# Attention sums on 32x32 tiles, with sequence quarter and head on the partitions and v kept on the chip

## The chip, the core and the metric

One core of a Trainium2 chip runs the kernel. Its engines work at the same time, each on its own instructions in their written order: TensorE (PE in the profile; its weight loads are shown as PEld), VectorE (DVE), ScalarE (ACT), GpSimd (POOL) and SyncE (SP), whose queue issues nearly all transfers. They meet through semaphores. The metric is the device time of one execution in microseconds; the time before is the median of three runs.

## What is computed

Two independent parts, whose outputs stand side by side in one result of 2048 x 1152, bfloat16. Part A is attention of 32 heads of 18 columns, in which each position looks at 8 earlier positions two apart (a window with dilation). Part B is a short convolution of k, a product with v, a causal convolution over the whole sequence (by a Fourier transform), and a product with q.

```python
def _A_ref(x, wqkv, wo):                   # x 1 x 2048 x 576
    H = 32; Dh = D // H; W, dil = 8, 2
    q, k, v = qkv[0], qkv[1], qkv[2]       # of x @ wqkv, by head
    idx = pos[:, None] - off[None, :]      # off = 0, 2, ..., 14
    mask = idx >= 0
    logits = jnp.einsum("bhsd,bhswd->bhsw", q, kg) * scale
    logits = jnp.where(mask[None, None, :, :], logits, -1e9)
    attn = _softmax(logits, axis=-1)
    o = jnp.einsum("bhsw,bhswd->bhsd", attn, vg)
    return o.transpose(0, 2, 1, 3).reshape(B, S, D) @ wo

def _B_ref(q, k, v, shift_k, ssm_k, ssm_D):
    # k_shift: 4 taps of shift_k over k; kv = k_shift * v
    # y: causal convolution of kv with ssm_k, by FFT of length 2 S
    y = y + kv * ssm_D[None, None, :]
    return q * y
...
return jnp.concatenate([a, b], axis=-1)
```

## The kernel before

**Order.** A string `ORDER` lists some 500 steps by short names with numbers, and a loop at the end calls the function of each; that is the order in which every engine and every queue gets its instructions. A suffix after a colon chooses the PSUM pool (`a` or `b`, two buffers of 2 x 512 fp32 each) and the engine that copies out of PSUM (`s` for ACT, `v` for DVE). So a step's place in the string decides what stands ahead of it on each engine, and an instruction that waits holds up what is behind it on its engine.

**Part A.** `load_x`, `x_tr` bring x in and transpose it on PE. `qk_step` and `qk_tail_step` project q and k, with the columns (head, element) on the partitions and all 2048 positions in the row. `v_step(c, k)` projects v for 512 positions in the same way, with 16 columns from the chunk before in front, and writes it to a DRAM buffer `Dv`; `v_load` reads it back with another layout: partition (head, j), where j = 0..3 is a window offset, and elements of v and positions in the row. Four of the eight windows lie in the partitions, the other two groups of four (`wg`) are made by an offset.

`l_mul(n, h)` multiplies q with shifted k on DVE (4096 elements in a row of each partition; the remaining 64 columns have products of 2048). `l_sum(n)` adds over the elements of a head with PE: a matrix `Eh` of zeros and ones, 32 columns wide, on one of four column tiles of the array (`tile_position=(0, 32 * j)`), so that partition (j, head) of `Lt` gets the logits of window j. `at_step` transposes these on PE so that positions lie on the partitions, `softmax(hf, k)` runs in twelve steps for each half of the sequence (maximum in three steps, difference, exponential on ACT, sum in three steps, reciprocal, conversion, product in two steps), `bt_step` transposes back. `p_mul(c, ct)` multiplies the weights with v for chunk c of 512 positions and four (for ct = 4 two) elements of each head; `p_sum(c, k)` adds over the windows with a matrix `I4` on column tiles, and `p_out(c, tt)` is the output projection with `wo`. The output of two `p_out` leaves in one transfer, from one of two staging buffers.

**Part B.** `load_k`, `load_v`, `sk_step`, `kv_conv` (on DVE, products and sums of 2304 elements), `x_part` and `k_part` (first stage of the transform on PE, results to DRAM buffers `Dx`, `Dk`), `w_load` (back from there), `x_spec` and `k_spec` (second stage, line 594), `g_prod` (the complex product on DVE, two products of 1152 elements for each of 16 steps, lines 615 and 616), `g_inv` (inverse, line 629, to `Dy`), `y_load`, `y_step` (last stage on PE, product with q on DVE, line 706, result out).

**Buffers.** All work areas are cut by hand from ten `Area` tiles, re-used as the kernel goes on. A `Ring` is a set of slots; a step that takes a slot waits for its last user. `evac` and `copy32` are the helpers that copy from PSUM: lines 103, 105 and 367 in the profile stand for all of them.

Of the kernel before, what the change touches and what calls it, by code (L numbers as in the profile page):

```python
# [18 lines left out]
lx.0 tj lx.1 lx.2 lwq.1 lwv wm.11 tv t0 xt.0.2:av sk:b lk.0 t2 xt.1.2:av lwq.0 xt.1.0:av xt.1.1:bv xt.0.0:s xt.0.1:bv  # L19
xt.2.1:s qk.1.1.1:bs xt.2.2:s t3 tw t1 lx.3 cv.0.0:a lv.1 lk.1 qk.1.1.0:bs cv.0.1:b cv.0.2:b cv.0.3:b qk.1.0.0:s  # L20
xt.2.0:as lv.0 v.0.1:b cv.0.4:b v.1.1:bs wt lk.3 v.0.0:a xt.3.0:s cv.0.5:b lk.2 cv.0.6:a cv.0.7:b cv.1.0 qk.0.1.0:b
xt.3.1:b t4 xt.3.2:as cv.1.1 lm.0.1 cv.1.2:b t5 cv.1.3:b qk.0.0.0:a sx.0.0:s qt.1:s cv.1.4:a lm.0.0 v.2.1:as lv.2
sx.1.0:a cv.1.5 cv.1.6 sx.0.1:b qt.0:b sx.0.2:a cv.1.7:a qk.0.1.1 sx.1.1 qk.0.1.3:b v.0.2:s v.1.2:bs lm.0.2 v.1.0:a
sx.1.2:b qk.1.0.1:bs sx.3.0:b cv.2.0:a qk.0.0.1:a v.3.1:a cv.2.1 sx.3.1 sx.2.0:s cv.2.2:a qt.3:as v.2.0:as qk.1.1.3:bs
sx.2.1:s cv.2.3:a lm.1.0 lb.0:a cv.2.4 cv.2.5:b v.2.2:bs cv.2.6 lm.1.1 v.3.2:av sx.2.2:b sx.3.2:b lv.3 cv.2.7:b
qk.0.1.2:a lb.1:b cv.3.0:b lm.2.2 cv.3.1 cv.3.2:b v.3.0:a qk.1.1.2:bs lm.2.1 qk.0.0.3:bs qk.1.0.3:bs lwo sx.4.0:a
cv.3.3:a lm.3.1 qt.2 sx.4.1:b sx.4.2 qk.0.0.2:as cv.3.4:b cv.3.5:b sx.5.0:b lm.2.0 qk.1.0.2 sx.5.1:a lb.2:bs cv.3.6
cv.3.7:a lm.6.0 at.0.0 lkn sx.5.2:av lm.4.2 ia:b lm.3.0 sx.6.0:as sx.6.1:as sx.6.2:s kt.3:b sx.7.0 sx.7.1:a sx.7.2:av
kt.1:bv lb.3:bs kp.1.0:bs kp.1.1:as lm.4.1 lm.4.0 kp.1.2:bs kp.3.0:s kt.0:as kp.3.1:b kp.3.2:s lm.6.2 kt.2:av lb.4:a
kp.0.0 kp.0.1:s lm.6.1 at.0.1 sm.0.0 xl.0 kp.0.2 kp.2.0:av lm.5.1 kp.2.1:s kp.2.2:bs kt.5:as kt.4:s sm.0.1 lb.6:a  # L30
kp.5.0:av kp.5.1:bs lm.5.0 sm.0.2 xl.1 kp.5.2:as kp.4.0:bs kt.6 kp.4.1:a kp.4.2:as sm.0.3 kt.7:s lb.5:s kp.6.0:as
xs.0.0:bv kp.6.1:a xl.2 kp.6.2:as kp.7.0:v kp.7.1:a kp.7.2 lm.7.0 sm.0.4 lm.7.1 xs.1.0:as sm.0.5 xs.0.1 xs.1.1:a
sm.0.6 lb.7:bs sm.0.7 kl.1 sm.0.8 kl.0 kl.3 ks.1.0:s sm.0.9 sm.0.11 sm.0.10 ks.1.1:as ks.0.0 gp.1.0 at.1.0:av vl.0.0
gp.1.1 bt.0.1:v ks.0.1:bs gp.0.0 ks.3.0:bs gi.1.0:as vl.0.1 xs.2.0:b xl.4 xs.2.1:as gp.0.1 xl.3 bt.0.0:bv at.1.1:b
vl.1.2 sm.1.0 ks.3.1:as kl.2 gi.1.1 pm.0.0 gi.0.0:s xs.3.0:a sm.1.1 vl.0.2 ks.2.0:b pm.0.1 xs.3.1:as sm.1.2 gp.3.0
vl.1.0 kl.4 sm.1.3 gi.0.1:bs gp.3.1 pm.0.2 xs.4.0:as gp.2.0 ks.2.1:b ps.0.0:a pm.0.3 sm.1.4 ks.4.0:b xl.7 gp.2.1 kl.7
gi.3.0:a ks.4.1:b gp.4.0 xs.4.1:as vl.1.1 gi.2.0:s pm.1.4 ks.7.0:a xl.5 pm.1.0 ps.0.1:bs ks.7.1:s vl.2.0 gp.4.1 pm.1.1
xs.5.0:as sm.1.5 sm.1.6 xs.7.0:b kl.6 kl.5 gi.2.1:a xs.7.1:bs ps.1.0:v xs.5.1:b ks.5.0:a vl.3.0 xl.6 gi.4.0 ps.1.2:a
gi.3.1:s vl.3.2 pm.1.2 gi.4.1:as ks.5.1:s pm.0.4 sm.1.7 gp.5.0 pm.1.3 sm.1.8 ps.0.2:bs gp.5.1 xs.6.0 yl.3 sm.1.9 yl.2
ps.1.1:a ks.6.0:s po.0.0:s xs.6.1:bs sm.1.10 gi.5.0:a gp.7.0 yl.0 vl.2.1 gi.5.1:bs gp.6.0 po.0.2:a sm.1.11 vl.2.2  # L40
gp.7.1 po.0.1 ys.3.0:v ys.3.1:v yl.1 bt.1.1:as bt.1.0 po.0.3:bs ks.6.1:bs pm.2.0 gi.7.0:as gi.7.1 gp.6.1 pm.2.1
gi.6.0:a po.1.0:bs pm.2.2 ps.2.0:a vl.3.1 gi.6.1:bs pm.2.4 ys.2.0:av ps.2.2:bs pm.2.3 ys.0.0:v ys.2.1:bs ys.0.1:as
po.1.2 ps.2.1:a po.1.1:b po.1.3:bs pm.3.4 pm.3.0 po.2.0 yl.6 yl.4 pm.3.1 po.2.1:s ps.3.0:b pm.3.2 ps.3.2:a po.2.2:b
pm.3.3 ys.6.0:as yl.5 ys.1.0:v ys.1.1:v ps.3.1:as ys.6.1:v po.2.3:v yl.7 po.3.0:a ys.5.0:bv ys.5.1:a po.3.1:b po.3.2:s
ys.4.0:v po.3.3:b ys.4.1:v ys.7.0:a ys.7.1:bs
# [4 lines left out]
def kernel(  # L50
# [62 lines left out]
    Dv = dram.tile([4 * D, VT], BF16, name="Dv")  # L113
# [40 lines left out]
    class Ring:  # L154
# [27 lines left out]
    wv = const.tile([128, 6, D], BF16, name="wv")  # L182

    r1, r2, r3, r4, r5, r6, r7, r8, r9, r10 = (
        Area(f"area{i}", n) for i, n in enumerate((18528, 16384, 5 * S, 2560, 5 * 2 * D, 19 * D, 28 * D, 2 * S, 3168, 4 * D)))
# [11 lines left out]
    Lt = r8.take(2, S)  # L197
    vTs = [[r9.take(2, VT) for _ in range(2)], [r9.take(2, VT), r10.take(2, VT)]]
    wqt = r10.take(5, 2, 64)
    vtl = [r10.take(272) for _ in range(2)]  # L200
    for r in (r1, r3, r4, r5, r6, r7, r9, r10):
        r.reset()
# [6 lines left out]
    ath = [r5.take(8, W, H) for _ in range(2)]  # L209
    smt = r5.take(1536)  # L210
    Pr = Ring(*[r1.take(2, 4, 512) for _ in range(3)])
    Ptr = Ring(r1.take(2, 2, 512))
    oTr = Ring(r9.take(2304), r1.take(2304))
    sAr = Ring(r1.take(2, D))
# [4 lines left out]
    Yr = Ring(r7.take(8, HD), r7.take(8, HD))  # L219
    qtr = Ring(*[r7.take(4, HD) for _ in range(4)])  # L220
    Pp = Ring(r4.take(4, 2, HD), *[r7.take(4, 2, HD) for _ in range(3)])
    r7.reset(20 * D)
    shr = r7.take(4 * D)[0:1]
# [3 lines left out]
    prr = Ring(*[mk.take(4, 2, 512) for _ in range(3)])  # L227
    phr = Ring(mk.take(4, 512), mk.take(4, 512))
    mk.reset()
    vSr = Ring(*[mk.take(8, VT) for _ in range(3)])  # L230
    vStr = Ring(mk.take(2, VT), mk.take(2, VT))
    mk.reset()
# [21 lines left out]
    def load_wv():  # L254
        nc.sync.dma_start(wv[:, 0:4, :], A_wqkv[0:512, 2 * D:3 * D].rearrange("(kb p) a -> p kb a", p=128))
        nc.gpsimd.memset(wv[0:64, 4:6, :], 0.0)
        nc.sync.dma_start(wv[64:128, 4, :], A_wqkv[512:576, 2 * D:3 * D])
# [9 lines left out]
    wot = wv  # L267
    wor = A_wo.rearrange("(h d) n -> h d n", d=DH)

    def load_wo():  # L270
        for r in range(4):
            nq = 5 if r < 2 else 4
            nc.sync.dma_start(wot[32 * r:32 * r + 32, 0:nq, :], wor[:, r:r + 4 * nq - 3:4, :])
        nc.gpsimd.memset(wot[64:128, 4, :], 0.0)
        for r in range(2):
            nc.sync.dma_start(wot[32 * r + 64:32 * r + 96, 5, :], wor[:, 16 + r, :])

    ones_f, ident_f, i4_f = mk.f32(128), mk.f32(128), mk.f32(32)
# [19 lines left out]
    def t_ident():  # L298
        nc.gpsimd.memset(ones_f, 1.0)
        affine_pair(ident_f, ones_f, pattern=[[1, 128]], cm=-1, base_lo=0, base_hi_minus=0)  # L300
        nc.vector.tensor_copy(ident[:], ident_f)
        affine_pair(i4_f, ones_f[:, 0:32], pattern=[[-4, 32]], cm=1, base_lo=0, base_hi_minus=3)
        nc.vector.tensor_copy(I4[:], i4_f)
# [79 lines left out]
    def v_step(c, k):  # L383
        ps = psa()
        r0 = D * c + 256 * k
        if k < 2:
            vT, nxt = vTs[k][c % 2], vTs[k][1 - c % 2]
            if c == 0:
                nc.gpsimd.memset(vT[:, :, 0:16], 0.0)
            project(ps, wv, (256 * k, 256 * k + 128), slice(512 * c, 512 * c + 512))  # L390
            evac(vT[:, :, 16:VT], ps[:])
            nc.sync.dma_start(Dv[r0:r0 + 256, :].rearrange("(u p) t -> p u t", p=128), vT)
            if c < 3:
                nc.gpsimd.tensor_copy(nxt[:, :, 0:16], vT[:, :, 512:VT])
            return
        vt, nxt = vtl[c % 2], vtl[1 - c % 2]
        if c == 0:
            nc.gpsimd.memset(vt[0:64, 0:16], 0.0)
        for kb in range(5):
            for hh in range(2):  # L400
                t0 = 512 * c + 256 * hh
                nc.tensor.matmul(ps[64 * hh:64 * hh + 64, 0, 0:256], wv[:, kb, 512:D], xT[:, kb, t0:t0 + 256],
                                 start=(kb == 0), stop=(kb == 4), tile_position=(0, 64 * hh))
        evac(vt[:, 16:272], ps[:, 0, 0:256])
        nc.sync.dma_start(Dv[r0:r0 + 64, 0:272], vt[0:64, :])
        nc.sync.dma_start(Dv[r0:r0 + 64, 272:VT], vt[64:128, 16:272])
        if c < 3:
            nc.gpsimd.tensor_copy(nxt[0:64, 0:16], vt[64:128, 256:272])

    def v_load(c, k):  # L410
        nd = 8 if k < 2 else 2
        dst = (vSr if k < 2 else vStr).get((c, k))
        sl = Dv[D * c + 8 * k:D * c + 8 * k + 1, 2:3]
        nc.sync.dma_start(dst.rearrange("p d t -> p (d t)")[:, 0:nd * VT - 8],
                          bass.AP(tensor=sl.tensor, offset=sl.offset, ap=[[DH * VT, 32], [DIL, 4], [1, nd * VT - 8]]))
# [93 lines left out]

    def block(n):  # L510
        return n // 2 % 2, n // 4, 2 * (n // 4) + n % 2

    def l_mul(n, h):
        wg, m, aq = block(n)
        o0 = PADL - DIL * (W - 1 - 4 * wg)
# [121 lines left out]
    def p_mul(c, ct):  # L637
# [5 lines left out]
        if ct % 2:  # L643
            vSr.drop((c, ct // 2))
# [110 lines left out]
```

## Time and profile before

| what | value |
| --- | --- |
| time, median of 3 runs | 233.52 us (232.54 to 233.6) |
| profiled execution, span | 233.3 us |
| instructions | 4423 |
| PE busy, matmuls | 196.2 us (84%), 1727 |
| PEld busy, weight loads | 112.5 us (48%), 1736 |
| DVE busy | 200.7 us (86%), 199 |
| ACT busy | 164.7 us (71%), 241 |
| POOL busy | 22.2 us (10%), 53 |
| DMA, all queues | 60.57 MB, mean 260 GB/s |
| mean granted TensorE clock | 0.954 |

The span runs from the first to the last instruction of the profiled execution. Busy time of an engine is the time in which at least one of its instructions ran; matmuls are pipelined, so many lie in the same microsecond, and the mean duration of one says little of what the next has to wait. In a row of a group the number behind x counts the instructions, then come the busy time in us and the mean of one in ns, and after the second bar the time that the engine stood idle just before them. In the 40 slices a digit is the busy share in tenths, 9 for 90% or more. In the rows of stretches each engine has its busy us and in brackets its instructions; the last three numbers are the granted clock, the share of DMA engine time and GB/s. In a timeline row the first number is the start in us from the span's start, the second the us to the end of the last of the merged instructions. In the rows of the chain the numbers are start and length in us.

### The profile page before, as it was taken

What the parts mean: (1) busy time and instruction counts of PE and PEld (TensorE: products, weight loads), DVE (VectorE), ACT (ScalarE), POOL (GpSimd) and SP (SyncE); (2) the same over time, 40 slices, a digit from 0 to 9 for tenths busy, and PEclk for the clock granted to TensorE, in tenths of its full rate; (3) what the DMA queues carried; (4) which work ended last, traced back from release to release, by engine and by line L of the source; (5) the groups of instructions that cost most, each with busy time, mean ns of one, the idle gap of its engine ahead of it and who ended that gap; (6) DMA issues with size and microseconds to landing.
All of it is one profiled execution on the core that took longest, in us unless ns stands there. A gap on an engine that the chain in (4) does not pass through costs nothing. (4 is left out here: it accounts for less than half of the span.)

```text
span 233.3 us, 4423 instructions
## 1 busy us (share of the span) xinstructions
PE 196.2 (84%) x1727; PEld 112.5 (48%) x1736; DVE 200.7 (86%) x199; ACT 164.7 (71%) x241; POOL 22.2 (10%) x53
## 2 busy tenths in 40 slices
PE   7899969999999977959873979668898979896981
PEld 2644524544544444545532456434564656564661
DVE  2679999989596999778969999999999999996533
ACT  2675739677754969487989789899999758535321
POOL 8001540110210110200000000000000010010100
PEclk9999999999999996779998599999999999997999
DMA  6999823451169589977996998999798999799586
GB/s 221 348 276 393 248 85 106 155 162 48 55 198 268 134 273 327 218 221 211 307 290 207 330 353 326 374 355 400 306 360 299 327 332 379 274 275 339 121 272 214
DMA packets 46965, 60.57 MB, mean 260 GB/s; under 512 B 2368, under 2 KB 40064, under 8 KB 45920
## 3 DMA queue, kind: packets, MB, share of 16 engines
q1 hardware_dynamic: 46254, 57.78, 75.5%
q0 software_dynamic: 688, 2.51, 4.6%
q8 instruction: 13, 0.21, 0.4%
q14 instruction: 8, 0.07, 0.1%
q10 hardware_dynamic: 2, 0.00, 0.0%
HBM read 38.98 MB, written 21.31 MB: 258 GB/s over the span
## 5 line engine op out<-in xcount | busy, mean ns | idle before, releaser
L103 ACT ACTIVATE area<-psB 128x576 bf16<-128x576 f32 (+7 forms) x122 | 85.2, 745 | 32.2 <-PE psB L381 7.6
L103 ACT ACTIVATE area<-psA 128x576 bf16<-128x576 f32 (+7 forms) x105 | 75.6, 760 | 30.7 <-PE psA L381 12.0
L519 DVE TENSOR_TENSOR area<-area 128x4096 bf16<-128x4096 bf16 x16 | 36.4, 2285 | 5.7 <-PE psA L540 3.3
L642 DVE TENSOR_TENSOR area<-area,area 128x4096 bf16<-128x4096 bf16 (+1 forms) x20 | 40.7, 2069 | 0.1
L381 PEld LDWEIGHTS <-area 128*128 128x128 bf16 x160 | 15.5, 98 | 20.0 <-issue 3.0
L594 PEld LDWEIGHTS <-W 128*64 128x64 bf16 x256 | 14.1, 113 | 22.0 <-issue 15.0
L484 DVE TENSOR_TENSOR area<-area,area 128x2304 bf16<-128x2304 bf16 x16 | 21.6, 1362 | 0.8 <-PE psB L456 0.6
L594 PE MATMUL psB<-area,W 128*64 128x288 bf16 x160 | 16.2, 299 | 6.9 <-DMA area<-Dk 3.9
L381 PE MATMUL psB<-area,area 128*128 128x512 bf16 x85 | 20.1, 379 | 0.3
L693 POOL DMA_DIRECT2D area<-in_B_q_dram x8 | 6.0, 747 | 142.8 <-DVE area L706 119.2
L381 PE MATMUL psA<-area,area 128*128 128x512 bf16 x67 | 16.1, 379 | 2.7 <-DVE area L367 2.5
L456 PE MATMUL psB<-area,T 128*128 128x384 bf16 x58 | 14.8, 346 | 2.9 <-ACT area L103 2.7
L456 PEld LDWEIGHTS <-T 128*128 128x128 bf16 x96 | 9.3, 104 | 15.1 <-issue 9.2
L486 DVE TENSOR_TENSOR area<-area,area 128x2304 bf16<-128x2304 bf16 x12 | 16.3, 1356 | 0.3
L629 PEld LDWEIGHTS <-IAt 64*128 64x128 bf16 x256 | 12.4, 94 | 6.9 <-issue 4.0
L680 PEld LDWEIGHTS <-area 128*128 128x128 bf16 x128 | 12.4, 100 | 5.8 <-issue 2.6
L381 PE MATMUL psA<-area,wv 128*128 128x512 bf16 x60 | 13.9, 379 | 0.0
L594 PE MATMUL psA<-area,W 128*64 128x288 bf16 x96 | 10.2, 310 | 4.1 <-ACT area L103 3.6
L381 PEld LDWEIGHTS <-wv 128*128 128x128 bf16 x80 | 7.6, 98 | 9.4 <-issue 0.6
L616 DVE TENSOR_TENSOR area<-area 128x1152 bf16<-128x1152 bf16 x16 | 12.0, 749 | 0.0
L615 DVE TENSOR_TENSOR area<-area 128x1152 bf16<-128x1152 bf16 x16 | 11.9, 746 | 0.0
L456 PE MATMUL psA<-area,T 128*128 128x384 bf16 x38 | 10.0, 364 | 1.8 <-ACT area L103 1.7
(132 smaller groups left out, 270.1 us busy)
## 6 DMA issues: line engine op xcount, KB each, us to landing
area<-Dv SPq DMA_DIRECT2D x8, 1054.0 KB, 8.0
Dx<-area SPq DMA_DIRECT2D x16, 288.0 KB, 3.6
Dk<-area SPq DMA_DIRECT2D x16, 288.0 KB, 3.5
area<-Dx SPq DMA_DIRECT2D x8, 576.0 KB, 5.7
area<-Dk SPq DMA_DIRECT2D x8, 576.0 KB, 5.3
Dy<-area SPq DMA_DIRECT2D x8, 576.0 KB, 4.6
area<-Dy SPq DMA_DIRECT2D x8, 576.0 KB, 7.0
out_dram<-area SPq DMA_DIRECT2D x16, 288.0 KB, 3.7
```

The costliest lines, as they stand in the source:

```text
L103: nc.scalar.activation(dst, src, ACT.Copy, **({} if scale is None else {"scale": scale}))
L381: nc.tensor.matmul(ps[:, u, :], w[:, kb, cols[u]:cols[u] + 128], xT[:, kb, t], start=(kb == 0), stop=(kb == 4))
L456: nc.tensor.matmul(ps[:, ri, 0:384], T1[:, ri, :], sf[:, 384 * ch:384 * ch + 384], start=True, stop=not extra)
L484: nc.vector.tensor_tensor(tB if k else tA, kfull[:, 4 * c + 3 - j:4 * c + 7 - j, :], skb[:, j, :].unsqueeze(1).to_broadcast([128, 4, D]), ...
L486: nc.vector.tensor_tensor(tA, tA, tB, ALU.add)
L519: nc.vector.tensor_tensor(prr.get((n, h)), q2[h][:, :, 512 * aq:512 * aq + 512].unsqueeze(1).to_broadcast([128, 4, 2, 512]), kv, ALU.mult)
L594: nc.tensor.matmul(ps[64 * hp:64 * hp + 64, im, 0:HD], W2[:, im, 8 * g + 2 * prl + hp].rearrange("p l f -> p (l f)"), Wt[:, 2 * prl + hp, ...
L615: nc.vector.tensor_tensor(P[:, 0:2], X, K, ALU.mult)
L616: nc.vector.tensor_tensor(P[:, 2:4], X, swap, ALU.mult)
L629: nc.tensor.matmul(ps[:, hp, 0:HD], IAt[r, tab, 4 * g + 2 * hv + u, :], Pp[(i, hv)][r, n, u, :], start=(n == 0), stop=(n == 3), tile_posit ...
L642: nc.vector.tensor_tensor(P, vv, Lt[:, :, 512 * c:512 * c + 512].unsqueeze(2).to_broadcast([128, 2, nd, 512]), ALU.mult)
L680: nc.tensor.matmul(ps[:, di, 0:288], oT[:, 512 * ct + 128 * tt:512 * ct + 128 * tt + 128], wot[:, ct, d0:d1], start=(ct == 0), stop=False)
```

## The change

The attention gets another layout. Partition (a, head), where a = 0..3 is a quarter of the sequence of 512 positions, holds logits, softmax and v; the eight windows lie in the row. `l_sum(n)` now makes window n for all four quarters. The transposes `at_step` and `bt_step` go, since softmax works in this layout (two halves of 256 positions of each quarter). `v_step(n)` projects two elements of all heads for all quarters, straight into a buffer `V`, from weights whose columns `perm_wv` has sorted by element (five POOL copies); `Dv` and `v_load` go, and `v_halo` fetches the 16 positions before each quarter from the partitions of the quarter before, in three transfers from buffer to buffer. `p_mul(c, ct)` works on 128 positions of each quarter and eight windows. `p_sum(c, k)` adds the eight windows in PSUM with 32x32 tiles of the array: quarter a on the tile's rows, element dd on its columns. `p_out` takes five blocks of 128 rows; of the last one half is zero. `g_prod` becomes one product. The order of all steps is new, with new choices of PSUM pool and copying engine.

```diff
-    r1, r2, ... 19 * D, 28 * D, 2 * S, 3168, 4 * D)))
+    r1, r2, ... 19 * D, 28 * D, 2 * S, 2560, 4 * D)))
...
+    V = r7.take(DH, VT)
+    Lt = r8.take(W, 512)
+    Pr = Ring(*[r1.take(W, 4, 128) for _ in range(4)])
...
+    def perm_wv():
+        for kb in range(5):
+            nc.gpsimd.tensor_copy(wv[:, kb], wvn[:, kb].rearrange("p (h d) -> p d h", d=DH))
...
-    def v_step(c, k):
...
+    def v_step(n):
         ps = psa()
+        for u in range(2):
+            for kb in range(5):
+                for a in range(4):
+                    nc.tensor.matmul(ps[32 * a:32 * a + 32, u, :], wv[:, kb, 2 * n + u, :], xT[:, kb, 512 * a:512 * a + 512],
+                                     start=(kb == 0), stop=(kb == 4), tile_position=(0, 32 * a))
+        evac(V[:, 2 * n:2 * n + 2, PADL:VT], ps[:])
...
+    def v_halo(g):
+        d = slice(6 * g, 6 * g + 6)
+        nc.sync.dma_start(V[32:128, d, 0:PADL], V[0:96, d, 512:VT])
...
-    def at_step(hf, wg):
-    def bt_step(hf, wg):
...
-            o = Lt[:, wg, 1024 * hf:1024 * hf + 1024].rearrange("p (b h j) -> p b h j", b=8, h=H)
-            nc.vector.tensor_tensor(o, L[:, :, 4 * wg:4 * wg + 4, :].rearrange("p b j h -> p b h j"), r, ALU.mult)
+            nc.vector.tensor_tensor(L, L, recb.unsqueeze(1).to_broadcast([128, W, 256]), ALU.mult)
...
-        nc.vector.tensor_tensor(P[:, 0:2], X, K, ALU.mult)
-        nc.vector.tensor_tensor(P[:, 2:4], X, swap, ALU.mult)
+        nc.vector.tensor_tensor(Pv, Xv.unsqueeze(2).to_broadcast([128, 2, 2, 2 * HD]), Kv.unsqueeze(1).to_broadcast([128, 2, 2, 2 * HD]), ALU.mult)
...
+        P = Pr.get((c, ct))[:, :, 0:nd]
+        o0 = PADL - DIL * (W - 1) + 128 * c
+        vs = V[:, 4 * ct:4 * ct + nd, o0:o0 + 128]
+        vv = bass.AP(tensor=vs.tensor, offset=vs.offset, ap=[vs.ap[0], [DIL, W], vs.ap[1], [1, 128]])
+        nc.vector.tensor_tensor(P, vv, Lt[:, :, 128 * c:128 * c + 128].unsqueeze(2).to_broadcast([128, W, nd, 128]), ALU.mult)
...
     def p_sum(c, k):
+        pss = [psum("a", 2, 512), psum("b", 2, 512)]
+        nd = 4 if k < 2 else 2
+        cts = (2 * k, 2 * k + 1) if k < 2 else (4,)
+        for u, ct in enumerate(cts):
+            P = Pr[(c, ct)]
+            for n in range(W):
+                for a in range(4):
+                    for dd in range(nd):
+                        r = slice(32 * a, 32 * a + 32)
+                        nc.tensor.matmul(pss[a // 2][32 * dd:32 * dd + 32, a % 2, 128 * u:128 * u + 128], I4[r, :], P[r, n, dd, :],
+                                         start=(n == 0), stop=(n == W - 1), tile_position=(32 * a, 32 * dd))
+            Pr.drop((c, ct))
+        for g, ps in enumerate(pss):
+            if k < 2:
+                evac(oT[:, 2 * k:2 * k + 2, 2 * g:2 * g + 2, :], ps[:, :, 0:256].rearrange("p a (u t) -> p u a t", u=2))
+            else:
+                evac(oT[0:64, 4, 2 * g:2 * g + 2, :], ps[0:64, :, 0:128])
```

The end of the new order, from the first sum of the third chunk on (`pm` is `p_mul`, `ps` `p_sum`, `po` `p_out`, `ys` `y_step`, `yl` `y_load`):

```
ps.2.0 pm.2.2 yl.4 pm.2.3 ys.0.1:as po.0.0:b po.0.1:a ys.1.0:as po.0.2:b pm.2.4 yl.6 ps.2.1 pm.3.0 po.0.3:a pm.3.1
ps.2.2 yl.7 ys.4.0:bs ys.1.1:as ys.4.1:as po.2.0:b pm.3.4 yl.5 po.2.1:b ps.3.0 po.2.2:b pm.3.2 pm.3.3 ps.3.2
ys.7.0:as po.2.3:b ys.7.1:b ys.6.0:as ps.3.1 ys.6.1:as ys.5.0:b po.3.0:a po.3.1:av ys.5.1:bs po.3.2:av po.3.3:b
```

## The prediction

> **What bounds the kernel now.** I read four views of the profiled execution in this order: the 40 slices, the stretches that I cut at DVE's own turning points (its first long product, the first `p_mul`, the end of the last `p_mul`), the groups of instructions, and the chain that ended last with the timeline of PE around single steps. First the slices and stretches:
>
> ```profile
> DVE  2679999989596999778969999999999999996533
> DMA  6999823451169589977996998999798999799586
> ```
>
> ```profile
> core 0: us, PE busy (x) PEld busy (x) DVE busy (x) ACT busy (x) POOL busy (x), PEclk, DMA share, GB/s
> 0.00:16.10 16.10, 14.03 (x89) 7.35 (x91) 8.29 (x30) 8.68 (x12) 5.15 (x23) 1.00 0.92 283
> 16.10:143.40 127.30, 110.71 (x852) 59.07 (x859) 115.24 (x97) 94.27 (x129) 14.05 (x26) 0.93 0.72 223
> 143.40:213.60 70.20, 57.61 (x682) 36.29 (x679) 69.69 (x63) 56.22 (x95) 2.23 (x3) 0.99 0.96 333
> 213.60:233.30 19.70, 13.82 (x112) 9.80 (x110) 7.45 (x11) 5.57 (x8) 0.75 (x1) 0.93 0.72 214
> ```
>
> From 16.1 to 213.6 us DVE has 115.2 + 69.7 = 184.9 us of work in 197.5 us: it waits 12.6 us in all, and in the third stretch 0.5 us. DVE sets the length there. DMA engines are busy 0.96 in that stretch too, but only what someone waits for counts. In the last 19.7 us nothing is full; there the chain counts:
>
> ```profile
> 205.75 5.31 DMA out_dram<-area
> 219.02 5.22 DMA out_dram<-area
> ```
>
> Two output transfers hold staging buffers for over 5 us each. So the time is 16.1 (head) + 184.9 + 12.6 + 19.7 = 233.3. The span, 233.3, lies 0.2 under the median of the runs, so I reckon in the span and add nothing.
>
> **The change on DVE.** Durations are the means of one of these groups:
>
> ```profile
> L581 DVE TENSOR_TENSOR area<-area 128x1024 bf16<-128x1024 bf16 x4 | 7.5, 1890 | 0.1
> L569 DVE TENSOR_TENSOR area<-area 128x2048 bf16<-128x2048 bf16 x2 | 2.4, 1214 | 0.0
> L616 DVE TENSOR_TENSOR area<-area 128x1152 bf16<-128x1152 bf16 x16 | 12.0, 749 | 0.0
> L615 DVE TENSOR_TENSOR area<-area 128x1152 bf16<-128x1152 bf16 x16 | 11.9, 746 | 0.0
> L484 DVE TENSOR_TENSOR area<-area,area 128x2304 bf16<-128x2304 bf16 x16 | 21.6, 1362 | 0.8 <-PE psB L456 0.6
> ```
>
> The softmax's last product wrote the four windows innermost (1890 ns for 1024 elements); it becomes one product of 2048 elements in rows for each half, like the subtraction of line 569: 4 x 1.89 - 2 x 1.21 = 5.1 us less. The other softmax steps keep their sizes. The transposes to and from softmax lose their copies, seven on DVE at 0.68 (line 367, 128x512): 4.8 less. `g_prod` makes one product of 2304 elements where there were two of 1152: 16 x (1.495 - 1.362) = 2.1 less. `l_mul` and `p_mul` keep 16 products of 4096 and 4 of 2048 each (2.28 and 1.22); their rows get shorter for `p_mul` (128 elements), which line 563 already has at the full rate (1024 in rows of 128: 688 ns), so nothing. New choices of engine: `y_step` multiplies out of PSUM twice instead of 12 times (0.752 against 0.452 each), 3.0 less; fewer transposed copies, 1.4 less; but the conversions of line 105 rise from 10 to 18, by the rows 952, 752, 1223 and 418 ns from 8.7 to 16.1: 7.4 more. Identity corners: 0.5 more. Sum: 8.5 us less, DVE 192.2. Of this 8.3 stay in the head, and 4.8 stand behind the last `p_mul` (six `y_step` products, two conversions), so 179.1 in the middle. With the same 12.6 of waits the last `p_mul` ends at 16.1 + 179.1 + 12.6 = 207.8. `t_w2` (2.4 us) moves behind the first convolutions, which were DVE's next work anyway; the first part of k has two transfers fewer before it. That may save up to 2.4 us and I count nothing.
>
> **The tail.** Behind the last `p_mul` PE has six halves of `y_step` (0.49 each in the chain), five `p_out` (ten matmuls, 1.22), and two sums (about 1.3): 10.3 us; then an evacuation, 0.7, and 3.6 from the last DVE operation to the end, as now: 14.6. With one wait like the two above it is 19.8. I take 17: 207.8 + 17 = 224.8.
>
> **Transfers.** Both ways through Dv, 2.4 MB written and 9.5 MB read, go. At 333 GB/s the reads fill 28 us of the third stretch, yet DVE and PE never waited for one; the waits for Dk, 3.9 us on PE, are what the relief can reach. 0 to 4, I take 0. Three halo transfers of 96 x 6 rows of 32 bytes come in on SP's queue. No row has such pieces; between 1.8 (the quickest landing into Dv) and 10 us (its slowest). Only `p_mul` of c = 0 reads what they bring, and the last two are issued some seven DVE operations (11 us) ahead: nothing, and up to 5 without that cover. `perm_wv` adds five POOL copies of 576 columns: between 0.59 (a 576-column memset) and 13 us each (the row of 32 columns at 713 ns, scaled). Some 15 convolution steps, over 20 us, lie between it and the first `v_step`, which with all PE work behind it would wait: nothing up to 4 us each, and I take the lower end, since a 32-column row is mostly start. With 13 it would be 40 us late.
>
> **PE, the open cost.** Unchanged: `v_step` has 360 matmuls of 512 columns on four column tiles, which start four in 0.215 us, 19.4 us, where 80 full ones and 40 half ones took 19.3. The 64 transposes go: eight in 0.44 us by their starts, 3.5 less. The sums change most: 128 matmuls of 512 columns and 32 of 256 (8.6 + 1.8 = 10.4 us) become 2304 matmuls of 128 columns on 32x32 tiles, each with a weight load: 4608 instructions where all of PE had 3463.
>
> ```profile
> L658 PE MATMUL psA<-area,I 128*32 128x512 bf16 x96 | 6.3, 381 | 0.2
> ```
>
> ```profile
> 60.27 0.40 PE L530 MATMUL psA<-area,Eh 128*32 128x512 bf16 x4
> 60.50 0.18 PE L535 MATMUL psA<-maskb,row 128*32 128x16 bf16 x4
> 60.53 1.03 PE L540 MATMUL psA<-area,Eh 128*32 128x512 bf16 x16
> 84.19 0.61 PE L552 MATMUL psA<-ident,area 128*128 128x128 bf16 x8
> ```
>
> Tiles do run side by side: 96 matmuls of 381 ns fill only 6.3 us. No row has 16 tiles at once, so both bounds. Below: a 128-column matmul occupies its tile 56 ns (line 552, (0.61 - 0.22) / 7), 16 tiles together, 160 rounds: 8.8 us. Above: the array waits for its instructions. No stretch of over 32 instructions goes quicker than line 540's, 32 in about 0.86 us, 27 ns each: 124 us. Nearest is line 535: its four matmuls and four loads are through in 0.03 us, under 4 ns each: 17 us. A short burst says little of 512 in a row, but it is the only row with short matmuls on tiles. I take 13, between it and the lower bound.
>
> Is that hidden? From its first `p_mul` DVE has 67.5 us to the end of the last one, with 0.5 of waits and the tail 85. PE had 57.6 + 13.8 = 71.4 there; less sums and transposes 60.1. Of 85, the last 4.3 are not PE's, and some 5 of waits on DVE and ACT will stay (now 18.5 with the end). So 15.6 us of sums hide under DVE; each further one adds itself, because `p_mul` needs the product buffers that the sums free. At 13 the forecast stays **225 us**; ACT, 5 us more to 170, is not full.
>
> [...]
>
> **Rivals.** (1) PE's instructions come too slowly, moderately: from 5.5 ns each (25 us, the point from which it is slower than now) to 12 (55 us): 235 to 265, at 8 ns 37 us and 246. For it: nothing shows short instructions sustained, and PE already has 84% of the span. Against: line 535. Chance 0.28. (2) They come at a pace near the slowest bound, 12 to 27 ns: 265 to 333; at 17 ns 78 us and 287. For it: line 540's 27 ns is all that is seen over more than 32. Against: that stretch is explained by 512 columns in the array. Chance 0.13. [...] (3) The new order gives back the DVE work: 20 `p_mul` waiting 0.45 us each for product buffers make 9 us, 234. For it: four buffers now serve what three and one did. Against: 0.5 us of waits now. Chance 0.07. (4) The same with more, 236 to 242, or POOL's copies late: 0.06.
>
> **Numbers.** Forecast 0.46, with its own range 218 to 232; rival 1 0.28, 2 0.13, 3 0.07, 4 0.06. A measurement of this kernel tells about 0.5%, so 232.3 to 234.7 is no change: 0.07 (rival 3). Faster 0.46, slower 0.47. The range runs from 218, where half the head and all of the Dk wait are gained, to 270, into rival 2: some 0.05 lies below and 0.12 above.
>
> **What would show it.** Right: the busy time of the sums near 13 us, DVE near 192 busy with under 15 of waits before its last `p_mul`, that one ending near 208. Wrong by rival 1 or 2: `p_mul` waits for the sums, a `p_sum` of 512 instructions lasts 3 us or more, DVE's share falls under 80%. Wrong by 3: the sums are short but DVE waits over 20 us. If POOL's copies are late, PE idles at the first `v_step`.

## The result, and the profile after

The changed kernel takes 282.53 us (median of 4 runs, 281.36 to 283.09), the kernel before 233.03 us beside it. The ratio is 1.2141, with a 95% interval of 1.2076 to 1.2206: a fifth slower, where 225 us was forecast. Some executions of a kernel fall into a slower state; times and ratios below are those of the others, while a profile can be of either. The profiled execution of the changed kernel has a span of 279.7 us and took 281.36.

First the 40 slices of the changed kernel:

```profile
PE   2999979999999577862896269799694487848593
DVE  6698999999999989987999352699557217280221
PEclk9999999999999999998698559999779559596868
```

Up to some 140 us DVE is as full as it was. Behind that it has holes, PE has them too, and the granted clock of PE falls to half in places. The stretches, cut at the same turning points as before (first long product of the convolution, first `p_mul`, end of the last `p_mul`):

```profile
0.00:14.60 14.60, 9.63 (x71) 6.63 (x72) 9.43 (x32) 7.11 (x11) 4.14 (x17) 1.00 0.90 279
14.60:141.70 127.10, 107.80 (x1060) 57.15 (x1057) 119.25 (x95) 93.22 (x122) 20.71 (x26) 0.97 0.57 184
141.70:250.70 109.00, 78.19 (x2426) 53.58 (x2423) 66.43 (x52) 60.17 (x109) 2.98 (x4) 0.80 0.56 174
250.70:279.70 29.00, 19.00 (x506) 13.50 (x505) 4.78 (x9) 7.94 (x14) 0.00 (x0) 0.74 0.25 80
```

The first two are 1.7 us shorter than in the kernel before. The third has grown from 70.2 to 109.0 us and the fourth from 19.7 to 29.0. In the third DVE has 66.4 us of work and 42.6 of waits, where it had 0.5. Transfers are not what it waits for: their share fell from 0.96 to 0.56. The view of line 608, the matmul in `p_sum`, says what is:

```profile
L608 PEld LDWEIGHTS <-I x2304: 87/94/146, 150.3 to 265.7; 32*32 32x32 bf16 x192
...
  issue: 64.3, 32
  ACT area L101: 1.7, 3
  DVE area L593: 0.2, 1
who waited for it (us, times):
  ACT area L101: 45.2, 12
  DVE area L593: 15.0, 3
```

Ahead of these instructions the two halves of PE (matmuls and loads, counted separately) stood idle 64.3 us with "issue", that is, waiting for nothing that the profile shows, and only 1.9 us for other engines. For the matmuls alone that is eleven halts with 30.6 us in all, and the sums' matmuls are busy for 26.3 us beside them. ACT then waited 45.2 us for the sums, and DVE 15.0 us directly. The timeline of PE through three halts, one row for some eight matmuls, idle time in brackets:

```profile
153.02 0.36 PE L608 MATMUL psA<-area,I 32*32 32x128 bf16 x7
157.51 0.28 PE L608 MATMUL psA<-area,I 32*32 32x128 bf16 x1 [4.13 <-issue]
...
158.73 0.33 PE L608 MATMUL psA<-area,I 32*32 32x128 bf16 x7
160.97 0.28 PE L608 MATMUL psA<-area,I 32*32 32x128 bf16 x1 [1.91 <-issue]
...
162.11 0.33 PE L608 MATMUL psA<-area,I 32*32 32x128 bf16 x7
164.70 0.28 PE L608 MATMUL psA<-area,I 32*32 32x128 bf16 x1 [2.26 <-issue]
```

Between two halts stand 128 matmuls and 128 loads, 256 instructions, started within some 1.2 us: under 5 ns for each. Then PE stands still, and the next 256 begin 3.46 and 3.73 us after the ones before. Counted in PE's order of instructions, all eleven halts of over 1.3 us with "issue" in or right behind the sums lie a multiple of 256 apart, to within one (instructions 2748, 3004, 3260, 4539, 5307, 5563, 5819, 6331, 6587, 7099 and 7867), though the steps around them differ. The page has a queue that carries instructions:

```profile
q8 instruction: 31, 0.51, 0.8%
```

31 packets of 16 KB; PE has 8110 instructions, and 8110 / 256 = 31.7. The trace also has the times of these packets, and the halts can be held against them. The stretch from 155.2 to 156.3 us, inside the first halt above, has one:

```profile
q8 instruction: 1, 0.02, 5.5%
```

It moves from 155.23 to 156.20 us, and PE goes on at 157.51; the next two move from 158.63 to 159.59 and from 162.11 to 163.31, and PE goes on at 160.97 and 164.70. The same holds for all eleven halts: one packet for each, and PE goes on 1.3 to 1.6 us after its end. The packet after that starts 1.0 to 1.5 us after PE has gone on. Those two waits and the packet's own 0.9 to 1.3 us make the 3.5 us. So in this trace PE's instructions arrive in blocks of 256, one in some 3.5 us, and a block of short ones is used up, in some 1.2 us, before the next is there.

The chain that ended last runs through the halts, and shows what follows them:

```profile
159.06 1.91 issue
...
162.44 2.26 issue
...
173.40 1.39 PE psA L627 x10
...
197.21 2.62 issue
...
200.65 2.51 PE psA L627 x10
```

Ten matmuls of a `p_out` take 1.39 us in one place and 2.51 right behind a halt: the granted clock was 1.00 during the first and 0.50 during the second. Over the whole third stretch it is 0.80, where the kernel before has 0.99.

### The profile page after: what moved, and what is told of

It reads as the page before. It is cut to its first block, busy times and chain, and to the rows that moved or that the text cites. A ratio compares the mean times of both kernels' runs of the same rounds, so it can differ in the third digit from the quotient of the medians.

```text
span 279.7 us, 8997 instructions
## 1 busy us (share of the span) xinstructions
PE 214.6 (77%) x4055; PEld 130.9 (47%) x4055; DVE 199.9 (71%) x183; ACT 168.4 (60%) x253; POOL 27.8 (10%) x47
## 3 DMA queue, kind: packets, MB, share of 16 engines
q0 software_dynamic: 688, 2.51, 3.3%
## 4 chain that ended last, share of the span: by engine, by line
PE 50%; ACT 15%; issue 14%; DMA 11%; DVE 8%; SPq 0%; ACTq 0%
ACT area L101 14%; PE psA L608 5%; PE psA L383 5%; PE psA L627 5%; PE psA L376 5%; PE psB L608 4%; PE psB L627 4%; DMA Dk<-area 3%; PE psB L376 3%; DVE area L461 3%; DVE area L463 3%; DMA area<-in_B_ssm_k_dram 3%; PE psA L647 3%; PE psB L383 2%; DMA area<-Dx 2%
## 5 line engine op out<-in xcount | busy, mean ns | idle before, releaser
L101 ACT ACTIVATE area<-psA 128x576 bf16<-128x576 f32 (+8 forms) x119 | 83.1, 738 | 72.3 <-PE psA L608 34.4
L608 PEld LDWEIGHTS <-I 32*32 32x32 bf16 x2304 | 21.8, 94 | 36.6 <-issue 35.3
L608 PE MATMUL psB<-area,I 32*32 32x128 bf16 x1152 | 25.5, 258 | 17.0 <-issue 16.8
L608 PE MATMUL psA<-area,I 32*32 32x128 bf16 x1152 | 25.6, 257 | 13.7 <-issue 12.3
L651 DVE TENSOR_TENSOR area<-area,area 128x576 bf16<-128x576 bf16 x14 | 6.4, 458 | 31.9 <-ACT area L101 31.7
L566 DVE TENSOR_TENSOR area<-area 128x2304 bf16<-128x2304 bf16 x16 | 21.2, 1350 | 8.0 <-ACT area L101 8.0
L376 PEld LDWEIGHTS <-area 128*128 128x128 bf16 x160 | 15.5, 98 | 18.0 <-issue 1.0
L627 PEld LDWEIGHTS <-area 128*128 128x128 bf16 x160 | 18.0, 114 | 9.8 <-issue 2.5
L376 PE MATMUL psA<-area,area 128*128 128x512 bf16 x90 | 20.6, 379 | 0.0
L376 PE MATMUL psB<-area,area 128*128 128x512 bf16 x70 | 16.2, 379 | 0.6 <-ACT area L101 0.6
L627 PE MATMUL psA<-wv,area 128*128 128x288 bf16 x80 | 15.1, 351 | 1.6 <-issue 1.5
L433 PEld LDWEIGHTS <-T 128*128 128x128 bf16 x96 | 8.7, 97 | 15.6 <-issue 7.9
L579 PEld LDWEIGHTS <-IAt 64*128 64x128 bf16 x256 | 12.5, 97 | 6.2 <-issue 2.5
```

The costliest lines, as they stand in the source:

```text
L101: nc.scalar.activation(dst, src, ACT.Copy, **({} if scale is None else {"scale": scale}))
L376: nc.tensor.matmul(ps[:, u, :], w[:, kb, cols[u]:cols[u] + 128], xT[:, kb, t], start=(kb == 0), stop=(kb == 4))
L566: nc.vector.tensor_tensor(Pv, Xv.unsqueeze(2).to_broadcast([128, 2, 2, 2 * HD]), Kv.unsqueeze(1).to_broadcast([128, 2, 2, 2 * HD]), ALU.mult)
L579: nc.tensor.matmul(ps[:, hp, 0:HD], IAt[r, tab, 4 * g + 2 * hv + u, :], Pp[(i, hv)][r, n, u, :], start=(n == 0), stop=(n == 3), tile_posit ...
L608: nc.tensor.matmul(pss[a // 2][32 * dd:32 * dd + 32, a % 2, 128 * u:128 * u + 128], I4[r, :], P[r, n, dd, :], start=(n == 0), stop=(n == W ...
L627: nc.tensor.matmul(ps[:, di, 0:288], oT[:, ct, a, :], wot[:, ct, d0:d1], start=(ct == 0), stop=(ct == 4))
```

## The experiments

Theory 1 is that the blocks set the pace: 256 instructions in some 3.5 us. Theory 2 is a cost of each instruction without blocks, theory 3 that the array, the order or the buffers are to blame. The first four runs tell these apart.

**The rates by themselves.** A kernel of nothing but matmuls, in stretches:

```diff
+        for i in range(512):
+            nc.tensor.matmul(**tile32(i, 512))      # then 256, 128 and 16 columns
...
+        for i in range(512):
+            nc.tensor.matmul(ps[:, 1, 0:128], src[:, 0:128], src[:, 0:128], start=True, stop=True)
+        for i in range(64):
+            for j in range(8):
+                nc.tensor.matmul(**tile32(8 * i + j, 128))
+            for j in range(3):
+                nc.tensor.matmul(ps[:, 3, 0:512], src[:, 0:128], src[:, 0:512], start=True, stop=True)
```

> Computes nothing of the reference (the output is zeros): it only measures PE. After 32 full matmuls of 512 columns, 512 matmuls on 32x32 tiles, 16 tiles in turn, of 512, then 256, 128 and 16 columns; 32 full ones; 512 full ones of 128 columns; then 64 times 8 tile matmuls of 128 columns and 3 full ones of 512. Every matmul has its weight load, so 512 matmuls are 1024 instructions, 4 blocks of 256. Theory 1 (PE runs out of instructions, which arrive in blocks of 256, one block in some 3.5 us): the four tile stretches last the same, about 14 us each, whatever their columns, with halts of 2 to 3 us at every 256 instructions; the full ones of 128 columns (56 ns each, 28.7 us in all, 7 us for a block) and the mixed stretch (0.72 us for 22 instructions, 8 us for a block) show no halts. Theory 2 (a fixed cost of each instruction): no halts, and every stretch of 1024 instructions lasts at least as long as the 16-column one. Theory 3 (the array with 16 tiles is slower than reckoned): the time goes with the columns, 512 four times as long as 128, no halts.

The timeline of PE, one row for each burst (lines 57, 59, 61 and 63 are the tiles with 512, 256, 128 and 16 columns, line 67 the full matmuls):

```profile
11.11 2.85 PE L57 MATMUL ps<-src 32*32 32x512 bf16 x191
16.05 2.55 PE L57 MATMUL ps<-src 32*32 32x512 bf16 x128 [2.09 <-issue]
20.06 3.65 PE L57 MATMUL ps<-src 32*32 32x512 bf16 x128 [1.45 <-issue]
...
31.24 1.99 PE L59 MATMUL ps<-src 32*32 32x256 bf16 x128 [2.01 <-issue]
34.97 1.99 PE L59 MATMUL ps<-src 32*32 32x256 bf16 x128 [1.74 <-issue]
...
45.33 1.47 PE L61 MATMUL ps<-src 32*32 32x128 bf16 x128 [1.99 <-issue]
49.06 1.47 PE L61 MATMUL ps<-src 32*32 32x128 bf16 x128 [2.26 <-issue]
...
59.97 1.19 PE L63 MATMUL ps<-src 32*32 32x16 bf16 x128 [2.54 <-issue]
63.70 1.19 PE L63 MATMUL ps<-src 32*32 32x16 bf16 x128 [2.54 <-issue]
...
76.87 28.75 PE L67 MATMUL ps<-src 128*128 128x128 bf16 x512
```

Bursts of 128 matmuls begin every 3.5 to 4.0 us, whether a matmul has 512 columns or 16: theories 2 and 3 have no such steps. The first burst of tiles has 191 matmuls: with the work before it that makes 447 instructions to the first halt, somewhat under two blocks, which had come in ahead: the first packet of the instruction queue moves only at 13.70 us. Here too PE goes on 1.2 to 1.5 us after the end of a packet at every halt. The third burst of 512 columns (20.06) fills 3.65 of its 4.0 us, at a granted clock of 0.50, so in that one PE itself is busy for nearly all of the time. The 512 full ones of 128 columns take 28.75 us without a halt, 7.2 us for a block. In the mixed stretch, 8 short tile matmuls and 3 long ones in turn, nothing halts either: line 70 there has the same short matmuls as line 61 and waits 0.0 us, against 7.9. So the price falls on long runs of short instructions, not on short instructions as such.

**One window of eight.**

```diff
-            for n in range(W):
+            for n in range(1):
...
-                                         start=(n == 0), stop=(n == W - 1), tile_position=(32 * a, 32 * dd))
+                                         start=(n == 0), stop=True, tile_position=(32 * a, 32 * dd))
```

> The sums take one window of eight, so 288 matmuls on tiles in place of 2304 (576 instructions in place of 4608); the other seven windows' products are made and not added. Theory 1 (instruction blocks): 16 blocks fewer, all halts in the sums go, DVE sets the length again, its last p_mul ends at 208 to 216 and the time is 225 to 236. Theory 2 (a cost of each instruction): the same, so this run does not tell 1 from 2. Theory 3 (the new order, the PSUM pools, late copies): the halts were only where the waiting showed, the time stays above 260.

228.6 us, ratio to before 0.9865 (0.9776 to 0.9955). DVE has 65.3 us of work in the 68.4 between its first and last `p_mul`; the last one ends at 211.5, the tail is 15.0. So 54 of the 282.5 us are the price of seven eighths of the sums, and the new order costs little by itself: theory 3 falls. Whether the price is one of blocks or of single instructions this run can't tell; the run of rates does.

**The same sums in longer matmuls.** In one run a tile sums two elements (256 columns), in the other four (512); the rows of `wo` are sorted to match. The second:

```diff
+                    for ct in cts:
+                        r = slice(32 * a, 32 * a + 32)
+                        nc.tensor.matmul(pss[a // 2][32 * ct:32 * ct + 32, a % 2, :], I4[r, :],
+                                         Pr[(c, ct)][r, n].rearrange("p d t -> p (d t)"),
+                                         start=(n == 0), stop=(n == W - 1), tile_position=(32 * a, 32 * ct))
...
-            nc.sync.dma_start(wot[32 * r:32 * r + 32, 0:nq, :], wor[:, r:r + 4 * nq - 3:4, :])
+            nc.sync.dma_start(wot[32 * r:32 * r + 32, 0:4, :], wor[:, 4 * r:4 * r + 4, :])
```

> Computes the reference. The same products and the same columns through the array, but a sum takes two elements, 256 columns, at once: 1280 matmuls in place of 2304. Theory 1 (instruction blocks): 10 blocks in place of 18, 8 x 3.5 = 28 us less of block time, of which some was hidden: 250 to 264. Theory 2 (a cost of each instruction, no blocks): about four ninths of the sums' cost go, 255 to 265, but without halts at every 256 instructions. Theory 3 (array bound by columns, or the order): no change, 279 to 284.

> Computes the reference. A sum takes four elements, 512 columns, at once, on 8 tiles: 768 matmuls in place of 2304, with twice as long evacuations on 64 partitions. Theory 1 (instruction blocks): 6 blocks in place of 18, up to 42 us less, of which some was hidden, and up to 7 us more on ACT: 235 to 255. Theory 2 (a cost of each instruction): likewise 235 to 255, without halts. Theory 3 (array or order): no change or slower, 279 and more, since only half as many tiles work at once.

| matmuls in the sums | their blocks | packets of instructions | time, us | ratio to before |
| --- | --- | --- | --- | --- |
| 2304 (the change) | 18 | 31 | 282.53 | 1.214 (1.208 to 1.221) |
| 1280 (pairs) | 10 | 23 | 244.88 | 1.055 (1.041 to 1.069) |
| 768 (fours) | 6 | 19 | 236.65 | 1.019 (1.010 to 1.029) |
| 288 (one window) | 2.25 | 16 | 228.6 | 0.987 (0.978 to 0.996) |

The first three pass the same columns through the array, and the time falls by 46 us: it goes with the count of instructions, while the array even has fewer tiles at work in "fours" (8 of 16). "Pairs" (median of two) came out some 5 us better than the lowest number of any theory; four halts of PE's matmuls still stand there, of 1.2 to 4.1 us. In "fours" they are nearly gone; the view of its line 608:

```profile
L608 PEld LDWEIGHTS <-I x512: 87/92/92, 152.5 to 222.8; 32*32 32x32 bf16 x171
...
  issue: 2.8, 8
  ACT area L101: 1.4, 2
who waited for it (us, times):
  ACT area L101: 6.9, 6
  DVE area L594: 0.5, 1
```

Issue 2.8 us in place of 64.3. The granted clock of its execution is 0.969, against 0.881 for the change.

**The copies of v's weights.** On the timeline of the changed kernel POOL sorts v's weights, and four products of DVE's convolution become longer:

```profile
27.66 9.46 POOL L254 COPY wv<-area 128x576 bf16<-128x576 bf16 x5 [22.72 <-DMA area<-in_A_wqkv_dram]
29.04 2.35 POOL L254 COPY wv<-area 128x576 bf16<-128x576 bf16 x1
35.91 1.22 POOL L254 COPY wv<-area 128x576 bf16<-128x576 bf16 x1
```

The first row is all five merged, the others are the second and the fifth copy alone.

```profile
25.39 1.36 DVE L465 TENSOR_TENSOR area<-area 128x2304 bf16<-128x2304 bf16 x1
26.67 3.64 DVE L461 TENSOR_TENSOR area<-area,area 128x2304 bf16<-128x2304 bf16 x2
30.34 2.26 DVE L463 TENSOR_TENSOR area<-area,area 128x2304 bf16<-128x2304 bf16 x1
32.64 2.26 DVE L461 TENSOR_TENSOR area<-area,area 128x2304 bf16<-128x2304 bf16 x1
34.82 1.21 DVE L103 CAST area<-psB 128x1024 bf16<-128x1024 f32 x1
35.96 2.38 DVE L463 TENSOR_TENSOR area<-area,area 128x2304 bf16<-128x2304 bf16 x1
38.38 1.36 DVE L461 TENSOR_TENSOR area<-area,area 128x2304 bf16<-128x2304 bf16 x1
```

The next two runs load the weights in strides where they lie, one on top of "fours" and one on top of "one window":

```diff
-    wvn = r8.take(5, D)
+    wvn = wv[:].rearrange("p k d h -> p k (d h)")
...
-            nc.gpsimd.tensor_copy(wv[:, kb], wvn[:, kb].rearrange("p (h d) -> p d h", d=DH))
...
-                    nc.tensor.matmul(ps[32 * a:32 * a + 32, u, :], wv[:, kb, 2 * n + u, :], ...
+                    nc.tensor.matmul(ps[32 * a:32 * a + 32, u, :], wvn[:, kb].rearrange("p (h d) -> p d h", d=DH)[:, 2 * n + u, :], ...
```

> Computes the reference. The kernel of the sums with 512 columns, and v's weights are read in strides where they lie, so the five POOL copies go. Theory: while POOL copied, four of DVE's convolution operations lasted some 0.9 us longer each, on the engine that sets the length of the first 140 us; without the copies all of them last 1.36 and the time falls by 3 to 4 us, from 236.6 to about 233. Rival: strided weight loads of 36-byte steps make v_step slower on PE, which is not the bound there: no change. Rival: DVE's longer operations have another cause (the transfers running then): they stay near 2.3 us and the time stays at 236 to 237.

> Adds one window of eight, like the second run, and has no POOL copies. If the prediction's other terms hold (DVE 8.5 us less than before, sums hidden), and the POOL copies were its second error, the time is 224 to 226; if something else in the new order costs, it stays at 228.

On "fours" the ratio to before goes from 1.019 to 1.0067 (1.0022 to 1.0112), 234.56 us, some 2 us less where 3 to 4 were expected; on "one window" from 0.9865 to 0.9663 (0.9595 to 0.9732), 224.70 us. DVE in the first of them, at the same place:

```profile
26.59 2.62 DVE L461 TENSOR_TENSOR area<-area,area 128x2304 bf16<-128x2304 bf16 x2
29.24 1.36 DVE L463 TENSOR_TENSOR area<-area,area 128x2304 bf16<-128x2304 bf16 x1
30.64 1.36 DVE L461 TENSOR_TENSOR area<-area,area 128x2304 bf16<-128x2304 bf16 x1
```

Every product lasts 1.36 again; the rival causes fall. In the trace of the change the second copy runs from 29.04 to 31.39 us, and the product beside it ends at 30.31, 1.1 us before the copy; the next product ends at 32.60, 1.2 us after the copy. By these times products and copies take turns, and both get longer (what they take turns at is not shown): the copies beside products last 2.35 us, while the fifth, which starts just before its product and waits for none, lasts 1.22. Each product loses 0.9 to 1.0 us, not much less than such a copy by itself. The cast out of PSUM beside the fourth copy (34.82) is not lengthened: it lasts 1.21 us, and 1.22 in the run without copies.

**Conversions from DVE to ACT.** On top of "fours" with strided weights, nine of the conversions that the new order gives to DVE go to ACT ("v.1:av" becomes "v.1:a", and so on):

> Computes the reference. As the kernel with 512 columns and strided weights, and nine conversions out of PSUM between 60 and 150 us (three of v, two of the logits, four of the first transform stages; 8.9 us by their rows) go from DVE to ACT. Theory (DVE sets the length of the first part, ACT has room): 3 to 8 us faster than without, 225 to 230. Rival (PE waits for PSUM buffers that ACT frees later, ACT becomes what the chain goes through): no change or slower, 232 to 238.

236.34 us, 1.0156 (1.0096 to 1.0217): no gain, rather 2 us lost. The stretch from the head to the first `p_mul`, with the conversions on DVE and then on ACT:

```profile
14.60:140.00 125.40, 109.14 (x1027) 60.95 (x1024) 113.38 (x92) 91.86 (x117) 4.91 (x8) 0.93 0.56 180
```

```profile
14.60:140.00 125.40, 106.88 (x1016) 62.05 (x1015) 103.60 (x82) 96.17 (x125) 4.91 (x8) 0.95 0.55 177
```

DVE has 9.8 us less to do and the first `p_mul` comes no sooner (143.1 us, against 142.0). PE is as full as DVE in this stretch, ACT little less, and the chain that ended last has 53% PE and 24% ACT in it and 2% DVE. The time is the rival's; its cause is argued from these shares and not shown.

**One product in g_prod, alone in the kernel before.**

```diff
-        nc.vector.tensor_tensor(P[:, 0:2], X, K, ALU.mult)
-        nc.vector.tensor_tensor(P[:, 2:4], X, swap, ALU.mult)
+        nc.vector.tensor_tensor(Pv, Xv.unsqueeze(2).to_broadcast([128, 2, 2, 2 * HD]), Kv.unsqueeze(1).to_broadcast([128, 2, 2, 2 * HD]), ALU.mult)
...
-            for n, tab in enumerate((0, 2, 1, 1)):
+            for n, tab in enumerate((0, 1, 1, 2)):
```

> Computes the reference. The kernel before with one part of the change: g_prod makes one product of 2304 elements in place of two of 1152 (16 x (1.495 - 1.352) = 2.3 us less on DVE, spread over its second half, where it waits for next to nothing). If DVE sets the length there, 1.5 to 2.3 us faster, 231 to 232; if transfers or PE do, no change.

The product's rows went from 23.9 to 21.3 us, and the time from 233.36 to 232.92 in the medians, with a ratio of 0.9985 (0.9949 to 1.0021): anything from 1.2 us less to 0.5 more. The full 2.3 us are excluded, and DVE's busy time says why: it fell by 0.9 us (200.7 to 199.8), not by 2.6. Neighbouring DVE instructions overlap in the rows (above, a product that starts at 32.64 and lasts 2.26 us ends at 34.90, and the cast behind it starts at 34.82), so the durations of two short ones add up to more than they keep the engine. Whether the 0.9 us arrive can't be told.

**Towards a version that is faster than both.** On top of "fours" with strided weights: a fifth buffer for the loads from Dx, Dk and Dy; then two of the loads from Dx ahead of a write to Dy in SP's order; then six `y_step` products straight out of PSUM.

```diff
+    r11 = Area("area10", 4 * D)
...
+    Wr.slots.append(r11.take(8, HD))
...
-gi.2.1:a xl.4 xs.6.0:b gi.1.0:a ks.6.1:b pm.0.1 kl.7 gp.1.1 po.1.0:a xs.6.1:b ks.5.0:a sm.1.7 xl.5 gi.1.1:b
+xl.4 gi.2.1:a xs.6.0:b xl.5 gi.1.0:a ks.6.1:b pm.0.1 kl.7 gp.1.1 po.1.0:a xs.6.1:b ks.5.0:a sm.1.7 gi.1.1:b
```

> Computes the reference. The kernel with 512 columns and strided weights, and a fifth buffer for what comes back from Dx, Dk and Dy, in the same order. In that kernel PE waits 5.9 us for a transfer from Dx at 166 us, and DVE behind it for 3.0 and 3.7 us. If the transfer starts late for want of a buffer, up to 6 us of it go: 229 to 234. If it starts late because SP's queue stands behind a write to Dy that waits for its evacuation, nothing: 234 to 236.

> Computes the reference. As the run with the fifth buffer, and two loads from Dx stand ahead of the write to Dy (of the one before) on SP's queue. If the queue was the cause, 3 to 6 us less than with the strided weights alone: 228 to 232. If transfers as such are late (they last 5 us however early), 233 to 235.

> Computes the reference. As the run with the early loads, and six y_steps multiply on DVE straight out of PSUM (0.75 us) in place of a copy on ACT (0.69) and a product (0.46): DVE 1.8 us more, ACT 4.1 less. If ACT's copies out of PSUM are what the chain runs through (a fifth of it), 1 to 3 us less; if DVE is, up to 2 us more.

The ratios to before are 0.9934 (0.9895 to 0.9974), 0.9900 (0.9850 to 0.9950) and 0.9894 (0.9847 to 0.9940). So the fifth buffer is worth some 3 us against "fours" with strided weights (1.0067); that the wait for Dx was what it took away is not shown, since its profile still has one in the chain, of 7.9 us (5.9 without the buffer). With the early loads that wait is gone from the chain, and one of 4.9 us for Dk stands in its place; neither that step nor the last can be told from the one before it. The last, 231.43 us, is 1.1% faster than the kernel before and some 18% faster than the change (231.43 / 282.53 = 0.82, from different sets of runs, so roughly).

## Why the prediction was wrong

**The step that failed is the price of the sums: "I take 13, between it and the lower bound."** PE's row pace, under 4 ns an instruction from line 535, was nearly right for a burst: 256 instructions in 1.05 to 1.2 us, 18 blocks, some 20 us; the sums' matmuls were busy for 26.3 us in all. What the sum of terms left out is that a run of such bursts is paced by the arrival of blocks, 3.5 us for 256 instructions or 13.7 ns each. The run with one window has 15.75 blocks fewer, 55 us at that pace, and is 54 us faster: next to nothing of them was hidden. In the change itself 30.6 of these us are the eleven halts, the rest is of the size of the bursts between them; the part of the low clock was not taken apart. The prediction had said that "a short burst says little of 512 in a row", and then took a value below the pace of that very burst. Its upper bound of 27 ns, 124 us, held.

**The rivals.** 282.5 us lies beyond the 270 at which the stated range ended, and in the second rival's 265 to 333 (chance 0.13), at its 12 to 27 ns. It had the cause in outline, instructions that come too slowly, but as a pace of each one, and that was not the mechanism: within a block they run at 4 to 5 ns, the run of rates has no fixed price of an instruction, and the mixed stretch shows the same short matmuls at no wait. The 17 ns that it reckoned 287 us from is shown by no run; in the runs the blocks came to 13.7 ns an instruction. The first test named in the prediction, "a `p_sum` of 512 instructions lasts 3 us or more", and DVE's share under 80% (71%) came out as for rivals 1 and 2.

**"15.6 us of sums hide under DVE" was probably too much.** From one window to "fours" PE's busy time rises by 11.3 us (187.1 to 198.4) and the time by 8; but longer evacuations on ACT are in it, so this is a sign and no proof. The halts came out whole: a halt holds the evacuation (ACT waited 45.2 us for the sums), the evacuation holds `p_mul` (DVE waited 15.0 us directly), and the PE work behind it starts late and at a lower clock (0.80 over the stretch, 0.99 before).

**The other terms held in part.** By the durations of their rows, the softmax product (7.5 us to 2.4), the transposed copies, `g_prod` (23.9 to 21.2) and the conversions (8.6 to 15.7) came as forecast; the identity corners cost 2.2 us more and not 0.5. Yet DVE's busy time went only from 200.7 to 199.9 us, where 192.2 was forecast. The largest part of this is the copies on POOL. Their duration, 1.2 to 2.4 us each, was inside the bounds and late for nobody, as forecast; but they lengthen DVE's products beside them by some 3.7 us, and the prediction looked only at who waits for POOL, not at who runs slower beside it. The corners add 1.7, and the rest, some 2 us, is of the size of the overlaps that the run with one product in `g_prod` shows; it was not worked out row by row. With both mistakes taken out, seven eighths of the sums and the copies, the time is 224.70 us, the forecast's 225, but in part by balance: DVE is busy for 195.4 us there, its last `p_mul` ends at 210.1 and not at 207.8, and the tail is 12.5 us and not 17, with the sums left at an eighth. So no other term was off by more than some 5 us, and 225 can't be had in this way. The tail, forecast at 17 us, is 15.0 with one window and 29.0 in the change, with halts of 4.9 us at its start and 3.1 in it, and a granted clock of 0.74. Dv's transfers, counted as nothing, were not priced by a run of their own.

## What to carry to other kernels

Count instructions as well as columns: in the change and in the run of rates, bursts of 256 PE instructions that the array got through in 1.2 to 2.6 us were paced by their arrival, 3.5 to 4.0 us for 256, and the profile showed it as "issue" at every 256th. The cure here was to make each matmul longer (512 columns, a third of the instructions, 46 us), not fewer columns; between longer work, in the mixed stretch of the run of rates, the same short ones waited 0.0 us in place of 7.9. And a helper engine's copies are to be priced also by what they do to the engine beside them: here 9.5 us of POOL copies cost DVE 3.7.

## What the hardware showed that was not expected

- In the run of rates PE's instructions came 256 at a time, in 3.5 to 4.0 us, with tiles of 16 to 512 columns alike. The page's count of instruction packets (31, 23, 19, 16) is about PE's instructions divided by 256 (31.7, 23.7, 19.7, 15.9), and at each halt of the change and of the run of rates PE goes on 1.2 to 1.6 us after such a packet has ended.
- Little came ahead: the first halt in the run of rates stands at PE's 447th instruction, the next at 703 and 959.
- Matmuls on many tiles did run side by side: in the run of rates 128 of 128 columns with their loads were started in 1.2 us, where 128 full ones took 7.2 (28.75 us for 512).
- Weight loads of 32 columns at steps of 36 bytes lasted 140 ns in "fours" with strided weights, against 97 in the change for columns side by side (360 of them in `v_step`, behind matmuls of 512 columns); with them, and without the copies on POOL, the ratio to before was 1.0067 in place of 1.019.
- While POOL sorted v's weights, DVE's products of the convolution and the copies took turns: 1.36 us became 2.3, and a copy of 1.22 became 2.35.
